# FC2's 64-row chunk as two stacked passes in three of seven products, and b2 added by GpSimd

## The chip, the core and the metric

The kernel runs on one core of a Trainium2 chip. The metric is the time of one execution on the device in microseconds. TensorE (PE, with its weight loads as PEld), VectorE (DVE), ScalarE (ACT), GpSimd (POOL) and SyncE (SP) run side by side, each through its own instructions in order; SP and GpSimd also issue transfers (DMA).

## The reference

Two layers, each of a linear-attention block A and a feed-forward block B, with the same weights in both layers, on 2048 tokens of width D = 640:

```python
x = A_x
for _ in range(2):
    x = x + A(layernorm(x), wqkv, wo)
    x = x + B(layernorm(x), w1, b1, w2, b2)

def B(x, w1, b1, w2, b2):          # D = 640, F = 1728
    h = relu(x @ w1 + b1)
    return (h * h) @ w2 + b2
```

## The kernel before

All matmuls that matter split their float32 operands into a high part (rounded to TensorE's fp32r format) and a low part (the rest), and add three products: high times low, low times high, high times high. `mm3` (line 473) writes this out; FC2 has it at line 1256. ScalarE makes the high part by a copy, VectorE the low part by a subtraction.

**Block B.** Tokens go in NG = 4 groups of 512. For each group FC1 (line 1174) makes 14 chunks of 128 hidden features; chunk 13 has only FL = 64 (1728 = 13 x 128 + 64). `act` puts the squared ReLU into the tile `R`, 128 partitions by 2 halves of the tokens by 2 halves of the chunks by KH = 7 chunks by 256 tokens. So half 1 of the chunks ends in the chunk of 64 rows; its rows 64 to 127 are zero except row 64, which is one (`ones_row`), and the matching row of the second weight matrix holds b2.

FC2 is one level of a Strassen-Winograd scheme on the halves of tokens, chunks and output columns: seven products in the order 1, 5, 6, 2, 7, 3, 4 (`ORDER`). Products 2, 3 and 4 take their weights from, or their activations as, the second half of the chunks, so their last chunk has 64 live rows. Each product goes through PAIRS = 4 units: units 0 to 2 hold two chunks, unit 3 one. `s_op` makes the sums of quadrants of `R` in place on VectorE. `u_hi` and `u_lo` write the high and low parts of a unit into one of five slots of `arena`. `fc2_step` (line 1246) does, for a unit and a tile of 128 tokens, three passes a chunk with 320 output columns; a unit of two chunks has 2 x 2 x 3 = 12 passes, unit 3 has 6, a product 42, a group 294. `fc2_add` adds a finished product to the residual tile `xr[t]` and stores it when it is complete.

**Weights.** In layer 0 the weights are split once and kept in device memory (`kept`), then loaded again for each group: a ring of six tiles `u` (`load_ring`, line 341), and tiles `uw` for unit 0 of each product, which stay (line 351). Class `Prep` does the splitting. For chunk pair p of w2, `load_t` loads chunk p (`a`) and chunk 7 + p (`b`); for the last pair `b` has 64 rows, the rest is zeroed by GpSimd and b2 is loaded into row 64 (line 257). `mix` lets GpSimd form the combinations (line 270), `high`, `low` and `store` split and store them. The last two pairs (`LATE_T`) are prepared during FC1 of layer 0's first group, from steps 0 and 1 on.

**The order of the work** is written out by hand. In block B the events of `at(group, step, f)` run after step `step`; steps 0 to 13 are FC1's chunks, 14 to 41 FC2's units, and events of one step run in the order in which they were entered. `single(g, i)` spreads the preparation of the next group's tile i over group g: loading pq (line 696), its division, the projection in FC1 (steps 4, 7, 10, 13), then `add` (residual and layer-norm statistics, whose last two operations are GpSimd's, lines 371 and 372), `store` (normalise, then a copy to device memory issued by GpSimd, line 405), and loading it back transposed. In layer 0's last group `side_last` loads layer 1's q/k weights (`load_kq`, line 201) and first tiles.

Of the kernel before, what the change touches and what calls it, by code (L numbers as in the profile page):

```python
# [8 lines left out]
F32 = mybir.dt.float32  # L9
R32 = mybir.dt.float32r  # L10
AF = mybir.ActivationFunctionType
ALU = mybir.AluOpType

P = 128
S, D, F = 2048, 640, 1728
# [5 lines left out]
FL = F - 13 * P  # L21
TG = 4
# [14 lines left out]
KH = 7  # L37
PAIRS = 4
ORDER = (1, 5, 6, 2, 7, 3, 4)
# [26 lines left out]
def kernel(  # L66
# [11 lines left out]
    nc = tc.nc  # L78
# [146 lines left out]
    for m in ORDER:  # L225
        for k in range(PAIRS):
            a, b = unit_range(k)
            keep((m, k), [P, 2, b - a, HD])

    class Prep:  # L230
# [20 lines left out]
        def load_t(self, p, at=None):  # L251
            a, b, q = at or (gtile("wa"), gtile("wb"), gtile("wq"))
            nc.sync.dma_start(a, w2[p * P : (p + 1) * P])
            n = P if p < KH - 1 else FL
            if n < P:
                nc.gpsimd.memset(b[n:], 0.0)
                nc.sync.dma_start(b[n : n + 1], b2.rearrange("(o n) -> o n", o=1))
            nc.sync.dma_start(b[:n], w2[(KH + p) * P : (KH + p) * P + n])
            return p, a, b, q

        def mix(self):
            self.raws += self.staged
            self.staged = []
            if not self.mixes:
                return
            p, a, b, q = self.mixes.pop(0)
            lo, hi = slice(0, HD), slice(HD, D)

            def sub(out, x, y, op=ALU.subtract):
                nc.gpsimd.tensor_tensor(out=out, in0=x, in1=y, op=op)  # L270

            sub(q[:, lo], a[:, hi], a[:, lo])
            sub(q[:, hi], b[:, hi], a[:, hi])
            sub(a[:, hi], q[:, hi], a[:, lo], ALU.add)
            self.raws.append(((p, (2, 3)), b, 2 * D))
            self.raws.append(((p, (5, 7)), q, 2 * D))
            self.raws.append(((p, (1, 6)), a, 2 * D))


            def last():  # L280
                sub(b[:, lo], b[:, lo], a[:, hi])

            self.then[p] = last
            self.raws.append(((p, (4,)), b, D))
# [13 lines left out]
        def low(self, n=1):  # L298
            for _ in range(min(n, len(self.halves))):
                key, u, hi, lo, raw = self.halves.pop(0)  # L300
                nc.vector.tensor_tensor(out=lo, in0=raw, in1=hi.bitcast(F32), op=ALU.subtract)  # L301
                self.done.append((key, u))
                if key[1] == (2, 3):
                    self.then.pop(key[0])()
# [231 lines left out]
    for layer in range(N_LAYERS):  # L536
# [6 lines left out]
        ap = sg.enter_context(  # L543
            tc.tile_pool(name=f"a_{layer}", bufs=1, side="left", reuse_waits="tile")
        )
# [73 lines left out]
        if layer == 0:  # L619
# [27 lines left out]
            for ps, a, b in runs:  # L647
                d = T4[0][:, 0, :, a * P : b * P]
                nc.vector.tensor_tensor(
                    out=d[:, 1], in0=ps[:, : (b - a) * P], in1=d[:, 0].bitcast(F32), op=ALU.subtract  # L650
# [16 lines left out]
            out=mask, in_=mask, compare_op=ALU.is_ge, fill=0.0, base=0,  # L667
# [495 lines left out]

        R = bp.tile([P, 2, 2, KH, HT], F32, name="R", tag="R", bufs=1)

        def ones_row(h):
            nc.gpsimd.memset(R[FL:, h, 1, KH - 1], 0.0)
            nc.gpsimd.memset(R[FL : FL + 1, h, 1, KH - 1], 1.0)

        x1_odd["tile"] = bp.tile([P, TG, D], F32, name="x1", tag="x1", bufs=1)  # L1170
        arena = tmp.tile([P, SLOTS, 2, 2, HT], R32, tag="T", name="arena", bufs=2)
        pTs = wtile("pTs").rearrange("p (b j n) -> p b j n", b=2, j=2)

# [56 lines left out]
        def unit(g, n):  # L1230
            q, k = divmod(n, PAIRS)
            a, b = unit_range(k)
            return quad(*QUAD[ORDER[q]], k), arena[:, (g * N_STEPS + n) % SLOTS, :, : b - a]

        def u_hi(g, n):
            v, u = unit(g, n)
            nc.scalar.activation(u[:, 0], v, AF.Copy)  # L1237

        def u_lo(g, n):
            v, u = unit(g, n)  # L1240
            nc.vector.tensor_tensor(out=u[:, 1], in0=v, in1=u[:, 0].bitcast(F32), op=ALU.subtract)  # L1241

        CHAIN = {1: (2, True, False), 6: (2, False, False), 7: (2, False, False), 4: (2, False, True),
# [2 lines left out]
        def fc2_step(g, n, i, first, last):  # L1246
            q, k = divmod(n, PAIRS)
            m = ORDER[q]
            base, opens, _ = CHAIN[m]
            _, u = unit(g, n)  # L1250
            w = wu.get(g, m, k).rearrange("p (j m n) -> p j m n", j=2, n=HD)
            ps = bank(base + i)[:, :HD]
            a, b = unit_range(k)
            for p in range(b - a):
                h, l = (u[:, j, p, i * P : (i + 1) * P] for j in range(2))
                for e, (x, y) in enumerate(((h, w[:, 1, p]), (l, w[:, 0, p]), (h, w[:, 0, p]))):
                    nc.tensor.matmul(  # L1257
                        ps, x, y, start=opens and k == 0 and p == 0 and e == 0,
                        stop=k == PAIRS - 1 and p == b - a - 1 and e == 2, skip_group_check=True,
                    )  # L1260

        ADD = {1: (0, 0), 5: (2, 1), 6: (0, 1), 2: (0, 0), 7: (2, 1), 3: (0, 1), 4: (2, 0)}
# [37 lines left out]
        def at(g, n, f):  # L1300
            events.setdefault((g, n), []).append(f)
# [19 lines left out]
        def single(g, i):  # L1321

            t, b = TG * (g + 1) + i, OUTS[i]

            def on(n, f):
                if n < 0 and g > 0:
                    at(g - 1, NF + N_STEPS + 2 * n, f)
                elif n >= NF:
                    at(g, NF + int(2 * (n - NF)), f)
                else:  # L1330
                    at(g, max(n, 0), f)

            if t > TG:
                on(b - 8, lambda: b_load_pq(t))
            on(b - 6, lambda: b_den(t))
            on(b - 5, lambda: b_blocks(t))
            on(b - 5, lambda: blocks_move(yzp[t], (0, 1)))
            on(b - 4, lambda: blocks_move(yzp[t], (2, 3)))
            sp = p_split(t)
            on(b - 3, lambda: next(sp, None))  # L1340
            on(b - 2, lambda: next(sp, None))
            on(b - 3, lambda: b_load_x(t))
            ps = []

            def out():
                yzp.pop(t)
                for j in range(2):
                    s = slice(j * HD, (j + 1) * HD)
                    ps.append(bank(6 + j)[:, :HD])
                    for c in range(DC):  # L1350
                        a = pT[t][:, :, c * P : (c + 1) * P]
                        mm3(ps[j], a[:, 0], a[:, 1], M[c][:, 0, s], M[c][:, 1, s], c == 0, c == DC - 1)
                pT.pop(t)

            def add():
                for j in range(2):
                    v = xr[t][:, j * HD : (j + 1) * HD]
                    nc.vector.tensor_tensor(out=v, in0=ps[j], in1=v, op=ALU.add)
                ln_stats(("b", t), xr[t])

            def store():
                xn[t] = ftile("xn")
                ln_apply(("b", t), xn[t], xr[t])
                xd[t] = spread_out(xn.pop(t))

            at(g, ("pe", b), out)
            on(b + 1 + 0.5 * (i == 3), add)
            on(b + 2, store)

            def load():  # L1370
                yzx[t] = spread_in(xd.pop(t))

            n = NF + (1, 5, 9, 13)[i]
            at(g, NF + (0, 3, 7, 11)[i], load)
            steps(lambda: x_split(t), (g, n + 4), (g, n + 5), (g, n + 6))

        def ffn_events(g):
            for k in range(PAIRS):
                at(g, 6 + k, lambda k=k: u_hi(g, k))
                at(g, 7 + k, lambda k=k: u_lo(g, k))  # L1380
            for k in range(3):
                at(g, 9 + 2 * k, lambda k=k: s_op(1, k))
            at(g, 11, lambda: u_hi(g, PAIRS))
            at(g, 12, lambda: u_lo(g, PAIRS))
            s = NF
            for h in range(2 if g == 0 else 1):
                at(g, 12 + h if g == 0 else 1, lambda h=h: ones_row(h))
            at(g, s, lambda: s_op(1, 3))
            for n in range(PAIRS + 1, N_STEPS):
                at(g, s + n - 4, lambda n=n: u_hi(g, n))  # L1390
                at(g, s + n - 3, lambda n=n: u_lo(g, n))
            for k in range(PAIRS):
                at(g, s + 3 + k, lambda k=k: s_op(2, k))
                at(g, s + 8 + k, lambda k=k: s_op(3, k))
                at(g, s + 13 + k, lambda k=k: s_op(4, k))
            for q in range(len(ORDER) - 1):
                for i in range(2):
                    at(g, s + PAIRS * (q + 1) + i, lambda q=q, i=i: fc2_add(g, q, i))
# [19 lines left out]
        def side_last():  # L1418
# [21 lines left out]
            for t in range(2):  # L1440
                at(g, s + 8 + 4 * t, lambda t=t: xT_split(t, turn(yz0[t], True)))

        for g in range(NG):
            ffn_events(g)
        for g in range(NG - 1):
# [63 lines left out]
```

## Time and profile before

| | us |
|---|---|
| median of 3 runs | 1326.48 (1326.28 to 1326.78) |
| the profiled execution | 1327.06 |
| its span, first to last instruction | 1325.3 |
| TensorE busy in the span | 1317.7 |
| VectorE, ScalarE, GpSimd busy | 848.4, 735.1, 167.2 |

All times below are from the profiled execution, counted from its first instruction. The granted TensorE clock was 1.00. In rows of groups the numbers are: operation, output and input tiles with shapes, count, then busy us in all and mean ns of one, then idle time in front of it and what ended it. In rows of the timeline: start us, us, engine, line. A row of waits gives us in all, times, longest. In rows of stretches: busy us of PE, PEld, DVE, ACT, POOL with counts, then granted clock, the DMA share (busy share of the 16 transfer engines) and GB/s.

### The profile page before, as it was taken

What the parts mean: (1) busy time and instruction counts of PE and PEld (TensorE: products, weight loads), DVE (VectorE), ACT (ScalarE), POOL (GpSimd) and SP (SyncE); (2) the same over time, 40 slices, a digit from 0 to 9 for tenths busy, and PEclk for the clock granted to TensorE, in tenths of its full rate; (3) what the DMA queues carried; (4) which work ended last, traced back from release to release, by engine and by line L of the source; (5) the groups of instructions that cost most, each with busy time, mean ns of one, the idle gap of its engine ahead of it and who ended that gap; (6) DMA issues with size and microseconds to landing.
All of it is one profiled execution on the core that took longest, in us unless ns stands there. A gap on an engine that the chain in (4) does not pass through costs nothing.

```text
span 1325.3 us, 20933 instructions
## 1 busy us (share of the span) xinstructions
PE 1317.7 (99%) x7525; PEld 1200.1 (91%) x7525; DVE 848.4 (64%) x1575; ACT 735.1 (55%) x1594; POOL 167.2 (13%) x263
## 2 busy tenths in 40 slices
PE   9999999999999999999999999999999999999999
PEld 8888889989988988998988899999899899889888
DVE  8888958757845854833856677686476558458045
ACT  5888967785475467334323233487844744754242
POOL 2333310122001001001012222000110010010000
PEclk9999999999999999999999999999999999999999
DMA  6898994499974985898954456554869569749756
GB/s 198 249 277 272 335 343 142 164 330 380 320 281 148 303 296 169 253 373 287 361 155 127 129 139 169 130 203 158 313 208 350 206 191 323 280 143 297 286 185 216
DMA packets 134751, 320.93 MB, mean 242 GB/s; under 512 B 16679, under 2 KB 61863, under 8 KB 134008
## 3 DMA queue, kind: packets, MB, share of 16 engines
q1 hardware_dynamic: 127416, 297.31, 66.9%
q0 software_dynamic: 7232, 22.29, 6.4%
q8 instruction: 60, 0.98, 0.3%
q14 instruction: 43, 0.35, 0.1%
HBM read 242.16 MB, written 65.54 MB: 232 GB/s over the span
## 4 chain that ended last, share of the span: by engine, by line
PE 85%; DVE 5%; ACT 4%; DMA 3%; issue 1%; SPq 1%; POOL 0%; ACTq 0%; DVEq 0%; POOLq 0%
PE PS L477 30%; PE PS L1257 25%; PE PS L1189 25%; PE PS L504 2%; ACT z L443 1%; PE PS L1030 1%; PE PS L1043 1%; ACT z L463 1%; DMA kq<-kept_kq 1%; DMA pqt<-pq 1%; DVE bn L367 1%; DMA kept<-uprep 1%; DVE uprep L301 0%; PE PS L837 0%; DVE xT L493 0%
## 5 line engine op out<-in xcount | busy, mean ns | idle before, releaser
L1189 PE MATMUL PS<-xTb,u 128*128 128x512 f32 x1640 | 377.1, 389 | 0.4 <-ACT arena L1237 0.3
L1189 PEld LDWEIGHTS PS<-xTb,u 128*128 128x128 f32 x1640 | 306.6, 188 | 63.6 <-ACT arena L1237 0.7
L477 PE MATMUL PS<-kq,xT 128*128 128x320 f32 (+2 forms) x1575 | 285.0, 334 | 1.5 <-DVE xT L493 1.4
L477 PEld LDWEIGHTS PS<-kq,xT 128*128 128x128 f32 x1575 | 250.3, 188 | 29.6 <-DVE xT L493 2.0
L1257 PE MATMUL PS<-u,arena 128*128 128x320 f32 x1692 | 257.2, 309 | 0.0
L1257 PEld LDWEIGHTS PS<-u,arena 128*128 128x128 f32 x1692 | 250.5, 188 | 0.0
L1241 DVE TENSOR_TENSOR arena<-R,arena 128x512 fp32r<-128x512 f32 x224 | 137.4, 617 | 145.6 <-ACT arena L1237 144.6
L1237 ACT ACTIVATE arena<-R 128x512 fp32r<-128x512 f32 x224 | 128.3, 575 | 177.0 <-PE PS L1257 168.0
L443 ACT ACTIVATE z<-y 32x160 f32<-32x160 f32 x512 | 171.1, 334 | 49.8 <-DVE y L434 43.9
L1200 ACT ACTIVATE R<-PS,b1sb 128x512 f32<-128x512 f32 x104 | 71.5, 687 | 131.2 <-PE PS L1189 130.3
L477 PE MATMUL PS<-kh,xh 128*128 128x512 f32 x480 | 124.8, 393 | 0.9 <-DVE kh L781 0.9
L477 PE MATMUL PS<-uM,pTs 128*128 128x320 f32 x720 | 109.4, 309 | 0.0
L477 PEld LDWEIGHTS PS<-uM,pTs 128*128 128x128 f32 x720 | 107.5, 188 | 1.9
L1257 PE MATMUL PS<-uw,arena 128*128 128x320 f32 x660 | 105.9, 309 | 0.0
L371 POOL TENSOR_SCALAR rs<-mv 128x1 f32<-128x1 f32 x64 | 34.8, 544 | 546.3 <-DVE mv L369 546.3
L477 PEld LDWEIGHTS PS<-kh,xh 128*128 128x128 f32 x480 | 87.1, 188 | 16.9 <-DVE kh L781 1.8
L1257 PEld LDWEIGHTS PS<-uw,arena 128*128 128x128 f32 x660 | 99.2, 188 | 0.2
L1218 DVE TENSOR_TENSOR R<-R 128x512 f32<-128x512 f32 (+1 forms) x128 | 78.2, 616 | 27.7 <-ACT R L1201 27.7
L463 ACT ACTIVATE z<-y 32x160 f32<-32x160 f32 x272 | 90.9, 334 | 3.3
L579 ACT ACTIVATE r<-PS 128x512 f32<-128x512 f32 (+1 forms) x64 | 27.6, 434 | 99.8 <-PE PS L477 98.6
L1270 DVE TENSOR_TENSOR x<-PS,x 128x320 f32<-128x320 f32 x112 | 53.6, 484 | 22.6 <-PE PS L1257 22.6
L1201 ACT ACTIVATE R<-R 128x512 f32<-128x512 f32 x104 | 65.8, 633 | 3.3
(129 smaller groups left out, 1209.9 us busy)
## 6 DMA issues: line engine op xcount, KB each, us to landing
u<-kept SPq DMA_DIRECT2D x113, 640.0 KB, 5.9
u<-kept_w SPq DMA_DIRECT2D x104, 640.0 KB, 5.6
u<-kept SPq DMA_DIRECT2D x56, 320.0 KB, 6.0
kept<-uprep SPq DMA_DIRECT2D x49, 320.0 KB, 5.9
z<-xb SPq DMA_DIRECT2D x160, 80.0 KB, 5.5
pqt<-pq SPq DMA_DIRECT2D x32, 320.0 KB, 6.0
acc<-r POOLq DMA_DIRECT2D x28, 320.0 KB, 5.2
uw<-kept SPq DMA_DIRECT2D x14, 640.0 KB, 8.7
```

The source lines that it names most:

```text
L371: nc.gpsimd.tensor_scalar(rs, mv[:, 1:2], LN_EPS, None, op0=ALU.add)
L443: nc.scalar.activation(zv[j * B32 : (j + 1) * B32, :, i, :], yv[i * B32 : (i + 1) * B32, :, j, :], AF.Copy)
L463: nc.scalar.activation(zv[j * B32 : (j + 1) * B32, :, i, :], yv[i * B32 : (i + 1) * B32, j], AF.Copy)
L477: nc.tensor.matmul(ps, a, b, start=first and i == 0, stop=last and i == 2)
L1189: nc.tensor.matmul(ps, a[:, d, :], bb[:, d, :], start=(d, i) == order[0], stop=(d, i) == order[-1],)
L1200: nc.scalar.activation(r, v, AF.Relu, bias=b1sb[:, c : c + 1])
L1201: nc.scalar.activation(r, r, AF.Square)
L1218: nc.vector.tensor_tensor(out=quad(*out, k), in0=quad(*x, k), in1=quad(*y, k), op=op)
L1237: nc.scalar.activation(u[:, 0], v, AF.Copy)
L1241: nc.vector.tensor_tensor(out=u[:, 1], in0=v, in1=u[:, 0].bitcast(F32), op=ALU.subtract)
L1257: nc.tensor.matmul(ps, x, y, start=opens and k == 0 and p == 0 and e == 0, stop=k == PAIRS - 1 and p == b - a - 1 and e == 2, skip_group_c ...
L1270: nc.vector.tensor_tensor(out=v, in0=ps, in1=v, op=ALU.add)
```

## The change

In products 2, 3 and 4 the last chunk's unit becomes one tile of 128 rows: rows 0 to 63 hold the high part, rows 64 to 127 the low part of the same 64 features. The weights of the second half of the chunks get the same 64 high rows twice, and their low tile gets zeros in rows 64 to 127. Two passes, stacked activations times low weights and stacked activations times high weights, then give the three products. Row 64 is no longer free for b2: the ones and the b2 row go, and b2 is loaded once per layer as a broadcast to 128 partitions (`b2bc`, SP) and added to the residual tile by GpSimd, one add of 128x640 for each of 16 token tiles a layer. Tiles of groups 1 to 3 get theirs three steps after their projection, those of group 0 at FC1 steps 4, 6, 8 and 10.

```diff
@@ load_t
                 nc.gpsimd.memset(b[n:], 0.0)
-                nc.sync.dma_start(b[n : n + 1], b2.rearrange("(o n) -> o n", o=1))
@@ mix
             sub(a[:, hi], q[:, hi], a[:, lo], ALU.add)
+            short = p == KH - 1
+            if short:
+                nc.gpsimd.tensor_copy(b[FL:], b[:FL])
...
             def last():
-                sub(b[:, lo], b[:, lo], a[:, hi])
+                if short:
+                    sub(b[:FL, lo], b[:FL, lo], a[:FL, hi])
+                    nc.gpsimd.tensor_copy(b[FL:, lo], b[:FL, lo])
+                else:
+                    sub(b[:, lo], b[:, lo], a[:, hi])
@@ low
-                nc.vector.tensor_tensor(out=lo, in0=raw, in1=hi.bitcast(F32), op=ALU.subtract)
+                if key[0] == KH - 1 and key[1] in ((2, 3), (4,)):
+                    nc.vector.tensor_tensor(
+                        out=lo[:FL], in0=raw[:FL], in1=hi[:FL].bitcast(F32), op=ALU.subtract
+                    )
+                    nc.gpsimd.memset(lo[FL:].bitcast(F32), 0.0)
+                else:
+                    nc.vector.tensor_tensor(out=lo, in0=raw, in1=hi.bitcast(F32), op=ALU.subtract)
@@ block B
-        def ones_row(h):
+        def no_rows(h):
             nc.gpsimd.memset(R[FL:, h, 1, KH - 1], 0.0)
-            nc.gpsimd.memset(R[FL : FL + 1, h, 1, KH - 1], 1.0)
+        b2bc = bp.tile([P, D], F32, name="b2bc", tag="b2bc", bufs=1)
+
+        def f_bias(t):
+            nc.gpsimd.tensor_tensor(out=xr[t], in0=xr[t], in1=b2bc, op=ALU.add)
...
+        def stacked(n):
+            q, k = divmod(n, PAIRS)
+            return k == PAIRS - 1 and ORDER[q] in (2, 3, 4)
@@ u_hi, u_lo
+            if stacked(n):
+                nc.scalar.activation(u[:FL, 0], v[:FL], AF.Copy)
+                return
...
+            if stacked(n):
+                nc.vector.tensor_tensor(
+                    out=u[FL:, 0], in0=v[:FL], in1=u[:FL, 0].bitcast(F32), op=ALU.subtract
+                )
+                return
@@ fc2_step
+                seq = ((h, w[:, 1, p]), (l, w[:, 0, p]), (h, w[:, 0, p]))
+                if stacked(n):
+                    seq = (seq[0], seq[2])
@@ single
             on(b + 2, store)
+            on(b + 3, lambda: f_bias(t))
@@ events, ahead of all others
+        at(0, 0, lambda: nc.sync.dma_start(
+            b2bc, bass.AP(tensor=b2.tensor, offset=b2.offset, ap=[[0, P], [1, D]])))
+        for t in range(TG):
+            at(0, 4 + 2 * t, lambda t=t: f_bias(t))
```

More of the change, by code (lines that the diff above doesn't have):

```diff
@@ L1255, in fc2_step @@
                 h, l = (u[:, j, p, i * P : (i + 1) * P] for j in range(2))
-                for e, (x, y) in enumerate(((h, w[:, 1, p]), (l, w[:, 0, p]), (h, w[:, 0, p]))):
+                seq = ((h, w[:, 1, p]), (l, w[:, 0, p]), (h, w[:, 0, p]))
+                if stacked(n):
+                    seq = (seq[0], seq[2])
+                for e, (x, y) in enumerate(seq):
                     nc.tensor.matmul(
                         ps, x, y, start=opens and k == 0 and p == 0 and e == 0,
-                        stop=k == PAIRS - 1 and p == b - a - 1 and e == 2, skip_group_check=True,
+                        stop=k == PAIRS - 1 and p == b - a - 1 and e == len(seq) - 1,
+                        skip_group_check=True,
                     )
@@ L1386, in ffn_events @@
             for h in range(2 if g == 0 else 1):
-                at(g, 12 + h if g == 0 else 1, lambda h=h: ones_row(h))
+                at(g, 12 + h if g == 0 else 1, lambda h=h: no_rows(h))
             at(g, s, lambda: s_op(1, 3))
```

## The prediction

> **What bounds the kernel now.** I read the page's busy table first, then who TensorE waited for, then the groups of instructions with shapes kept apart, then the chain of work that ended last, and the time-ordered views of the places where a gain could be lost.
>
> ```profile
> span 1325.3 us, 20933 instructions
> PE 1317.7 (99%) x7525; PEld 1200.1 (91%) x7525; DVE 848.4 (64%) x1575; ACT 735.1 (55%) x1594; POOL 167.2 (13%) x263
> ...
> PE PS L625 <- POOL ident masks.py:199: 1.4, 1, 1.4
> PE PS L477 <- DVE xT L493: 1.4, 2, 1.2
> PE PS L477 <- DVE kh L781: 0.9, 2, 0.5
> PE PS L1189 <- ACT arena L1237: 0.3, 1, 0.3
> ...
> L1257 PE MATMUL PS<-u,arena 128*128 128x320 f32 x1692 | 257.2, 309 | 0.0
> L1257 PE MATMUL PS<-uw,arena 128*128 128x320 f32 x660 | 105.9, 309 | 0.0
> ...
> 320.19 43.12 PE PS L1257 x294
> 880.77 13.22 PE PS L504 x90
> ```
>
> TensorE is busy 1317.7 of 1325.3 us and all its listed waits add up to 4.0 us. FC2 (line 1257) has 1692 + 660 = 2352 matmuls, 294 for each of 8 token groups, and no idle time in front of any. In a group the 294 take 43.12 us: 146.7 ns for one pass. So this stage is paced by the number of passes, and a pass that goes is worth 146.7 ns as long as what feeds TensorE keeps up.
>
> **The passes removed.** Unit 3 of products 2, 3 and 4 (the single 64-row chunk) is now two passes instead of three, for two token tiles: 3 x 2 = 6 passes a group, 48 in all. 48 x 146.7 ns = 7.04 us, 0.88 us a group, 0.29 us for each such unit. The two passes left have the same stationary tile one after the other; line 504 does that already (each high or low half meets two column halves) at 13.22 / 90 = 146.9 ns, so a pair costs what two others do. As the last group ends the program, its 0.88 us counts in full too.
>
> **Engines around the stacked unit.** The ScalarE copy and the VectorE subtraction handle 64 rows by 256 instead of 128 by 256. Duration follows the columns (64x512 and 128x512 both take 0.68 us below), so I cost both at zero change. New is that the first pass needs the VectorE half as well, where it needed ScalarE's alone. What hides this is the lead over TensorE:
>
> ```profile
> L1207 DVE SCALAR_TENSOR_TENSOR R<-R 64x512 f32<-64x512 f32 x8 | 5.5, 683 | 0.3
> L1218 DVE TENSOR_TENSOR R<-R 128x512 f32<-128x512 f32 x96 | 65.5, 683 | 27.7 <-ACT R L1201 27.7
> ...
> 324.28 0.63 POOL L405 DMA_DIRECT2D xb<-xn  x1 [1.48 <-DVE xn L377]
> ...
> 342.47 0.65 DVE L1241 TENSOR_TENSOR arena<-R,arena 128x512 fp32r<-128x512 f32 x1
> ...
> 320.00:363.00 43.00, 43.00 (x295) 43.00 (x294) 36.23 (x67) 16.51 (x30) 2.03 (x5) 1.00 1.00 316
> ```
>
> Unit 17 of the first group (fifth product, second unit) is finished by VectorE at 343.12; TensorE starts it at 320.19 + 4 x 6.16 + 1.76 = 346.59 (12 passes are 1.76 us, a product of 42 is 6.16). That is 3.47 us of lead in the fullest FC2 stage (VectorE 36.23 of 43 us). A stacked unit takes 0.29 off it. Cover gone, VectorE's delay would go to TensorE one for one.
>
> **The adds on GpSimd.** 32 adds of b2, 128x640 each. The nearest rows:
>
> ```profile
> L778 POOL TENSOR_TENSOR acc<-acc,r 128x640 f32<-128x640 f32 x2 | 3.6, 1818 | 16.3 <-DMA acc<-r 9.0 <-DVE r L587 7.3
> L773 POOL COPY acc<-r 128x640 f32<-128x640 f32 x2 | 1.8, 906 | 69.7 <-DVE r L587 69.7
> L1168 POOL MEMSET R<- 1x256 f32 x10 | 3.3, 328 | 0.6
> L256 POOL MEMSET R<- 64x640 f32 x1 | 0.6, 628 | 0.1
> ...
> 273.41 2.68 POOL L270 TENSOR_TENSOR R<-R 128x320 f32<-128x320 f32 x3
> 275.32 1.45 DVE L301 TENSOR_TENSOR uprep<-R,uprep 128x640 fp32r<-128x640 f32 x1 [2.90 <-ACT uprep L295]
> L301 DVE TENSOR_TENSOR uprep<-st,uprep 128x640 fp32r<-128x640 f32 x13 | 10.6, 818 | 0.8 <-ACT uprep L295 0.6 <-DMA wa<-in_B_w_dram 0.2
> ```
>
> Same shape and kind: 1.82 us, so 58 us for 32. Ten memsets (3.3 us) go; two copies of the weight preparation (0.9 and, at half the columns, about 0.45 us) and two memsets (0.6 and 0.3) come. GpSimd goes from 167 to about 224 us, idle for most of the span, so its own time is free; queued behind an add are only the layer-norm pair, the copy of the normalised tile to memory and the last mixes, one FC1 step later. The price can be on VectorE. At 275.32 a VectorE subtraction met GpSimd's mixes, which ran to 276.09, and took 1.45 us instead of 0.82: 0.63 lost in 0.77 us of overlap. So an add can hold VectorE for nearly its 1.82 us. In the six FC2 stages with an add (after the copy at 324.28 in the first) that is less than 3.47 - 0.29 us of lead: zero. In FC1 VectorE idles about half of the time and does not feed TensorE directly: zero, except in layer 0's first group.
>
> That rule is also in the Trainium skill (SBUF — State Buffer, § SBUF: two separate sides): the port pair shared by the two engines is an exclusive lock, held for a whole instruction, and whoever comes second blocks fully. The trace agrees, with 0.63 of 0.77 us. For the add's length the GPSIMD Engine Reference (§ Performance versus the Vector engine) has about 2.6 cycles an element at 1.2 GHz, an estimate of 1.39 us for 640; the measured 1.82 us decides, and with 1.39 the loss of the next part would be 2 x 0.43 = 0.9 us smaller at its upper end.
>
> **Layer 0's first group.** Here the weights are still being prepared and everything is tight:
>
> ```profile
> SPq L257 <- POOL R L256: 6.3, 1, 6.3
> ...
> 258.05 0.41 SPq L696 DMA_DIRECT2D pqt<-pq  x1
> ...
> 284.64 0.51 SPq L696 DMA_DIRECT2D pqt<-pq  x1
> ...
> 288.47 0.74 ACT L295 ACTIVATE uprep<-R 128x640 fp32r<-128x640 f32 x1
> ...
> 290.17 0.87 POOL L270 TENSOR_TENSOR R<-R 128x320 f32<-128x320 f32 x1 [2.58 <-DVE uprep L301]
> ...
> 294.02 0.82 DVE L713 TENSOR_TENSOR pr<-pqt,zbc 128x640 f32<-128x640 f32 x1 [2.32 <-DMA pqt<-pq]
> ...
> 313.28 2.52 PE L1189 MATMUL PS<-xTb,u 128*128 128x512 f32 x10 [0.34 <-ACT arena L1237]
> ...
> 265.00:270.00 5.00, 5.00 (x23) 4.13 (x22) 1.27 (x3) 4.86 (x11) 2.35 (x4) 1.00 0.62 212
> 285.00:320.00 35.00, 34.63 (x184) 30.30 (x183) 21.17 (x39) 26.20 (x58) 7.11 (x12) 1.00 1.03 411
> 900.00:974.00 74.00, 74.00 (x396) 65.81 (x395) 42.31 (x81) 52.04 (x120) 8.11 (x17) 1.00 0.65 233
> ```
>
> Removed with the b2 row is a transfer that held SP for 6.3 us until a GpSimd memset was done; the two loads behind it start earlier, into a stretch that is not yet saturated (share 0.62 from 265 to 270). But the next loads wait for VectorE and ScalarE anyway, so I give it nothing. Added is the broadcast of b2, 320 KB, at 411 GB/s 0.8 us of a path that is full (share 1.03) from 285 on; it is issued just ahead of the load at 258.05, some 27 us before that, so probably free. The mix of the last chunk pair comes 2.7 us later (an add and a copy ahead of it): ready near 278.8, needed by ScalarE at 288.5. Then the mix at 290.17, a copy and two adds keep GpSimd until about 290.17 + 0.87 + 0.5 + 2 x 1.82 = 295.2. VectorE's work from 294.02 on, which the chain follows into TensorE's 0.34 us wait at 313.28, may start 1.2 us late. Bounds: the wait vanishes (gain 0.34), or 1.2 + 0.8 = 2.0 us lost. I take 0.5 lost, nearer the gain's end since loads that start earlier work against it. In layer 1's first group the same adds stand beside a data path with a third to spare (share 0.65): zero.
>
> **The layer boundary.**
>
> ```profile
> 624.34 34.33 PE PS L1257 x234
> 658.68 0.32 SPq L341
> ...
> 659.53 10.00 DMA kq<-kept_kq
> 669.58 1.67 PE PS L477 x6
> ...
> 640.00:670.00 30.00, 29.94 (x199) 29.18 (x198) 19.56 (x37) 8.50 (x15) 0.00 (x0) 1.00 0.96 353
> ```
>
> The last q/k weight tile of layer 1 is issued at 659.53, right after TensorE freed a slot at 658.66, and lands at 669.53; TensorE takes it at 669.58. It lands just in time. In the changed kernel one stacked unit lies before the issue (0.29 us earlier), three before the use (0.88 earlier). So TensorE waits 0.88 - 0.29 = 0.59 us that it did not. Bounds: 0 (it lands faster) and 0.88 (the path, 0.96 busy, sets the landing). I take 0.59.
>
> **The sum.** 7.04 - 0.59 - 0.5 = 5.95 us gained. The profiled execution lasted 1327.06 us (1.76 around its span), so 1321.1; the median of the runs shown is 0.58 lower, so 1326.48 - 5.95 = 1320.5. With the terms' ends: 7.04 + 0.34 = 7.4 gained, or 7.04 - 0.88 - 2.0 = 4.2, so 1319.1 to 1322.3.
>
> **Rivals.** (a) Memory sets the pace where its share is near 1.00: in layer 0's first and last FC2 the passes only turn into waits for weights. Those 2 x 0.88 us go, and with 2.0 us lost in the first FC1 the gain is 7.04 - 1.76 - 2.0 = 3.3: 1323.2. For it: shares of 1.00 and 0.96. Against: the four waits above name no weight load in FC2.
>
> (b) Slower: in the six FC2 stages with an add, GpSimd keeps VectorE out longer than the lead. One add, at 1.82 us, does not; it decides from 3.2 us on, and from 3.2 + 7.04 / 6 = 4.4 us the kernel is slower. If an add between back-to-back two-operand subtractions takes three times its length, 5.5 us, TensorE loses 2.3 us six times: 13.8 - 7.04, 1333.2. For it: VectorE runs without a gap there. Against: mixes kept their 0.88 us beside VectorE at 273 to 276.
>
> (c) It does not do what it says: FC2 is paced by units, not passes, so fewer passes only leave TensorE waiting for ScalarE and VectorE: 1326.5. For it: these work only about four units ahead. Against: 0.0 idle in both rows of line 1257, and a product of short and long units advances at 146.7 ns a pass.
>
> **How the numbers follow.** Forecast 0.74, with its own range 1319.1 to 1322.3; (a) 0.14; (b) 0.06; (c) 0.06. The range for 8 in 10 takes in (a): 1318.9 to 1323.3. A measurement here tells about 0.2%, 2.65 us, from no change: faster is below 1323.8, which is the forecast and (a), 0.88; same is (c), 0.06; slower is (b), 0.06.
>
> **What will show it.** Right: each FC2 stage has 288 matmuls and takes 42.24 +- 0.1 us, with no idle time in front of its matmuls; GpSimd's adds show near 1.8 us; the wait before the layer-1 q/k matmuls grows to about 0.6 us, and the one in layer 0's first FC1 to about 0.8. Wrong: FC2 stages that stay at 43 us (then (c)), TensorE waits on weight loads inside FC2 (a), or TensorE waiting for VectorE's arena halves a few us after an add (b).

## The result, and the profile after

The changed kernel takes 1320.20 us (median of 6 runs, 1319.74 to 1320.73), the kernel before beside it 1326.46 us (6 runs, 1326.22 to 1327.84): ratio 0.9951, 95% interval 0.9939 to 0.9964. The profiled execution lasted 1320.5 us, 6.56 us less than that of before.

From the page of the changed kernel the span, the busy table and the two groups of FC2's matmuls (now line 1287):

```profile
span 1318.5 us, 20882 instructions
PE 1310.7 (99%) x7477; PEld 1193.5 (91%) x7477; DVE 865.5 (66%) x1575; ACT 735.5 (56%) x1594; POOL 219.1 (17%) x289
...
L1287 PE MATMUL PS<-u,arena 128*128 128x320 f32 x1644 | 250.2, 309 | 0.0
...
L1287 PE MATMUL PS<-uw,arena 128*128 128x320 f32 x660 | 106.1, 309 | 0.0
```

The view of TensorE's waits (us in all, times, longest) has four rows; the three of 1.4, 1.4 and 0.9 us outside FC1 and FC2 are as before, and one is new in it:

```profile
PE PS L489 <- DMA kq<-kept_kq: 0.2, 1, 0.2
```

TensorE has 48 matmuls less and still no idle time that the groups show in front of FC2's. The 0.3 us in FC1 for which ScalarE was named is gone, 0.2 us for the last q/k tile of layer 1 has come. The wait for that tile is not new, though: the list of the matmuls leaves out most of what their weight loads (PEld) wait. The waits of the weight loads for it, from 600 to 670 us, first before and then after:

```profile
PEld PS L477 <- DMA kq<-kept_kq: 0.5, 1, 0.5
```

```profile
PEld PS L489 <- DMA kq<-kept_kq: 0.6, 1, 0.6
```

VectorE is busy 17.1 us longer although it has the same 1575 instructions.

The chain of waits of the changed kernel (start, length, what ran) shows the stages around layer 0's first FC1 and around the layer boundary:

```profile
255.52 17.02 PE PS L1204 x75
...
306.18 9.09 PE PS L1204 x40
...
319.67 42.24 PE PS L1287 x288
...
621.17 34.24 PE PS L1287 x232
...
656.27 9.57 DMA kq<-kept_kq
665.88 1.67 PE PS L489 x6
```

FC2 of a group is 288 passes in 42.24 us, 0.88 us less than before. The last 10 of the 40 matmuls that close layer 0's first FC1 are not set off from the others any more. Set against the same places of before, stage by stage on TensorE:

| where | before, us | after, us | gained |
|---|---|---|---|
| FC2, 8 stages, passes alone | 8 x 43.12 | 8 x 42.24 | 7.04 |
| FC1 of layer 0's first group | 65.02 | 64.15 | 0.87 |
| start of the program to that FC1 | 253.58 | 253.93 | -0.35 |
| last FC2 of layer 0 and first part of layer 1 | 286.28 | 285.77 | 0.51 (0.88 of it counted above: -0.37) |
| end of the last FC2 to the end of the span | 3.27 | 3.65 | -0.38 |
| around the span | 1.76 | 2.0 | -0.25 |

The 0.37 us at the layer boundary have two parts. In time order, matmuls of that FC2 (start, length, line, count) and VectorE beside them:

```profile
639.49 1.92 PE L1287 MATMUL PS<-uw,arena 128*128 128x320 f32 x12
...
645.35 2.12 PE L1287 MATMUL PS<-uw,arena 128*128 128x320 f32 x12
```

```profile
643.84 0.83 DVE L505 TENSOR_TENSOR xT<-y,xT 128x640 fp32r<-128x640 f32 x1 [0.80 <-ACT xT L502]
...
645.79 0.48 DVE L1301 TENSOR_TENSOR x<-PS,x 128x320 f32<-128x320 f32 x1
```

The same twelve passes take 0.20 us more at 645.35, and between 600 and 670 us the one wait of a weight load in FC2 is for VectorE's addition of line 1301, 0.2 us. So this FC2 takes 42.44 us. The place lies right behind the first stacked unit, that of product 2. TensorE comes to it 0.29 us earlier, and the addition starts 645.79 - 621.17 = 24.62 us into the stage, where before it was 648.70 - 624.34 = 24.36, so 0.26 later. A stacked subtraction costs VectorE more than its duration shows. The same window of VectorE, a subtraction of 128x256 and one of 64x256 with what follows each:

```profile
648.60 0.42 DVE L1268 TENSOR_TENSOR arena<-R,arena 128x256 fp32r<-128x256 f32 x1
648.93 0.42 DVE L1233 TENSOR_TENSOR R<-R 128x256 f32<-128x256 f32 x1
...
651.98 0.42 DVE L1264 TENSOR_TENSOR arena<-R,arena 64x256 fp32r<-64x256 f32 x1
652.43 0.49 DVE L1301 TENSOR_TENSOR x<-PS,x 128x320 f32<-128x320 f32 x1
```

Both last 0.42 us, but the next instruction starts 0.33 us after the first and 0.45 us after the second. In this trace all 24 stacked subtractions start 0.03 us or more after the end of the instruction before and are over 0.03 us before the next begins. Where nothing has to be waited for, most of the 128x256 ones overlap their neighbours by about 0.08 us instead. That is 0.1 us more on each side. The six traces of kernels that stack product 2 all have this wait of 0.20 us, with and without the adds (experiment 2), and the six others have not.

The other part is the wait for the q/k tile: its first use comes 665.88 - 663.61 = 2.27 us after the end of FC2, before it was 669.58 - 667.46 = 2.12, so 0.15 more. This part scatters from kernel to kernel: the weight load waits 0.48 us for the tile before and 0.64 after (the 0.5 and 0.6 above), 0.43 in experiment 2, 0.17 in 3 and 8, and not at all in 1, 4, 5, 6 and both kernels of 7, of which 4, 5 and 6 have the changed FC2.

Together 7.04 + 0.87 - 0.35 - 0.37 - 0.38 - 0.25 = 6.56 us. The spans are given to 0.1 us, so the last two rows hold to about 0.05.

### The profile page after: what moved, and what is told of

The parts are those of the page before. It is cut to its first block, busy times and chain, and to the rows that moved or that the text cites. A ratio compares the mean times of both kernels' runs of the same rounds, so it can differ in the third digit from the quotient of the medians.

```text
span 1318.5 us, 20882 instructions
## 1 busy us (share of the span) xinstructions
PE 1310.7 (99%) x7477; PEld 1193.5 (91%) x7477; DVE 865.5 (66%) x1575; ACT 735.5 (56%) x1594; POOL 219.1 (17%) x289
## 4 chain that ended last, share of the span: by engine, by line
PE 91%; ACT 2%; DVE 2%; DMA 2%; SPq 1%; issue 1%; POOL 0%; ACTq 0%; DVEq 0%; POOLq 0%
PE PS L489 32%; PE PS L1204 28%; PE PS L1287 25%; PE PS L516 3%; ACT z L475 1%; PE PS L1042 1%; PE PS L1055 1%; DMA kq<-kept_kq 1%; SPq L246 1%; PE PS L849 0%; PE PS L637 0%; DMA xt<-in_A_x_dram 0%; DMA kept<-uprep 0%; DVE xT L505 0%; DVE r L599 0%
## 5 line engine op out<-in xcount | busy, mean ns | idle before, releaser
L1287 PE MATMUL PS<-u,arena 128*128 128x320 f32 x1644 | 250.2, 309 | 0.0
L1287 PEld LDWEIGHTS PS<-u,arena 128*128 128x128 f32 x1644 | 243.4, 188 | 0.0
L1268 DVE TENSOR_TENSOR arena<-R,arena 128x512 fp32r<-128x512 f32 (+1 forms) x200 | 140.8, 707 | 135.3 <-ACT arena L1259 134.8
L1259 ACT ACTIVATE arena<-R 128x512 fp32r<-128x512 f32 (+1 forms) x200 | 117.9, 593 | 157.9 <-PE PS L1287 131.9
L598 DVE TENSOR_SCALAR r<-r 128x512 f32<-128x512 f32 (+1 forms) x64 | 21.3, 332 | 70.4 <-ACT r L591 70.2
```

The source lines that it names most:

```text
L1287: nc.tensor.matmul(ps, x, y, start=opens and k == 0 and p == 0 and e == 0, stop=k == PAIRS - 1 and p == b - a - 1 and e == len(seq) - 1, s ...
```

## The experiments

Ten kernels were run, each beside the kernel before on the same chip, in this order of questions: which half of the change gains, whether the gain follows the passes, what an add costs, and what lies behind the small terms of the table.

**1. The bias alone.** Three passes for every unit, b2 by the broadcast and GpSimd's adds:

```diff
-            short = p == KH - 1
+            short = False
...
-                if key[0] == KH - 1 and key[1] in ((2, 3), (4,)):
+                if False:
...
-            return k == PAIRS - 1 and ORDER[q] in (2, 3, 4)
+            return False
```

> Three passes everywhere again, b2 still by broadcast and GpSimd adds. Theory (the gain is the 48 passes and nothing else of size): FC2 stages are back at 294 matmuls in 43.12 us, and the time is that of the kernel before less the 0.34 us wait in layer 0's first FC1: 1326.1 us (1325.8 to 1326.5). Rival 1 (moving b2 out of the matmul brings part of the gain itself, through SP and the removed memsets): below 1324.5. Rival 2 (the adds cost time by locking VectorE out): above 1327.

Measured: 1326.95 us against 1326.25, ratio 1.0006 (0.9998 to 1.0015), above the range expected; of the 0.7 us more, the end of the program and the time around the span account for about 0.6 (experiment 8). Seven FC2 stages take 43.12 us again. The first FC1 still takes 64.15 us, so this gain comes without any stacking; FC2 right behind it takes 43.69 us. From the chain of waits of this kernel:

```profile
339.48 8.53 DMA u<-kept
348.15 15.20 PE PS L1287 x102
...
427.49 43.12 PE PS L1287 x294
```

The weights that are needed at 348 hold TensorE's weight loads for 0.57 us, and the stage is longer by as much: in this execution a late transfer took back one stage later most of what FC1 had saved. Moving b2 gains nothing by itself.

**2. The stacking alone.** Neither broadcast nor adds; b2 is left out of the result:

```diff
         def f_bias(t):
-            nc.gpsimd.tensor_tensor(out=xr[t], in0=xr[t], in1=b2bc, op=ALU.add)
+            return
...
-        at(0, 0, lambda: nc.sync.dma_start(
-            b2bc, bass.AP(tensor=b2.tensor, offset=b2.offset, ap=[[0, P], [1, D]])))
```

> The changed kernel without the broadcast load and without the 32 adds: b2 is left out of the result. Theory (adds are off the path): within 0.3 us of the changed kernel, 1320.2 us, though VectorE's busy time falls back by about 17 us to that of the kernel before (848). Rival (the adds hold VectorE and through it TensorE, or the broadcast delays loads): 1 us or more faster than the changed kernel, below 1319.2.

Measured: 1319.63 us against 1326.25, ratio 0.9950 (0.9938 to 0.9963). FC2 takes 42.24 us as in the changed kernel, and 42.44 at the layer boundary, also as there. The b2 row's load is gone here too, but leaving out that load alone gains nothing (experiment 7), so the whole gain is the stacking's. The gain is 6.62 us here and 6.26 with the adds and the broadcast: they cost some 0.4 us on top (0.6 between the two medians, taken on different chips), a little more than the 0.3 us expected, and it does not lie in FC2. VectorE's busy time falls back to 851.1 us, where about 848 was expected.

**3. One product stacked in place of three.**

```diff
-            return k == PAIRS - 1 and ORDER[q] in (2, 3, 4)
+            return k == PAIRS - 1 and ORDER[q] == 3
```

> Only product 3 stacked: 16 passes fewer instead of 48. Theory (146.7 ns for each pass that goes): 2.35 us from the passes, 0.34 from the first FC1, a loss of up to 0.2 at the layer boundary: 1326.46 - 2.5 = 1324.0 us; FC2 stages of 292 matmuls in 42.83 us. Rival (FC2 is paced by units, or the gain comes from elsewhere): not in proportion, either 1326 or already near 1321.

Measured: 1324.65 us, ratio 0.9988 (0.9979 to 0.9997), 0.65 us above the forecast: 16 passes give 2.35 us, of which 0.41 at the end and 0.32 around the span (experiment 8) are lost again, and 1.60 us were measured. The chain of waits of this kernel up to its first FC2:

```profile
304.56 8.02 DMA u<-kept_w
312.72 2.51 PE PS L1204 x10
...
319.62 42.83 PE PS L1287 x292
```

Two passes less are 43.12 - 42.83 = 0.29 us, so the stage follows the passes: 294, 292 and 288 give 43.12, 42.83 and 42.24 us. The stage is not paced by units. And the FC2 at the layer boundary takes 42.82 us, without the 0.20 us that is lost there behind product 2's stacked unit: product 3 comes after that place. The first two rows bear on the open point of experiment 7: they name the transfer of a weight tile that lands at 312.58 and holds the last ten matmuls of FC1.

**4. Three adds in place of one.** Add, subtract, add again, for one token tile of each of six groups, so that GpSimd keeps at it for three times as long in six FC2 stages:

```diff
-            nc.gpsimd.tensor_tensor(out=xr[t], in0=xr[t], in1=b2bc, op=ALU.add)
+            n = 3 if t >= TG and t % TG == 3 else 1
+            for i in range(n):
+                op = ALU.subtract if i % 2 else ALU.add
+                nc.gpsimd.tensor_tensor(out=xr[t], in0=xr[t], in1=b2bc, op=op)
```

> Changed kernel with the add that falls into FC2 (fourth tile of the next group, six stages) done three times: add, subtract, add. Each stage then has 4.8 us of GpSimd adds instead of 1.6. Theory L1 (an add bars VectorE for its whole length and the next add follows at once): VectorE's subtraction for unit 6 is 5.2 us late, 0.4 us over its lead of 4.8, and the following work goes on being late: 0.4 to 1.5 us lost in each of six stages, 1322.5 to 1329. Theory L2 (VectorE gets one instruction in between two adds): the lead shrinks by about 2 us at the first and by less than the lead in all; TensorE does not wait, 1320.2 us.

Measured: 1324.65 us against 1326.68, ratio 0.9983 (0.9974 to 0.9993). Six FC2 stages take 42.93 to 42.96 us, 0.70 more than with one add, the other two stay as they were. First what one add does in the changed kernel, in order of time (start, length, engine and line, what):

```profile
322.13 0.69 DVE L1268 TENSOR_TENSOR arena<-R,arena 128x512 fp32r<-128x512 f32 x1 [0.54 <-ACT arena L1259]
...
323.89 2.67 DVE L1268 TENSOR_TENSOR arena<-R,arena 128x512 fp32r<-128x512 f32 x1 [0.54 <-ACT arena L1259]
...
324.41 1.59 POOL L1185 TENSOR_TENSOR x<-x,b2bc 128x640 f32<-128x640 f32 x1
...
326.48 0.68 DVE L1233 TENSOR_TENSOR R<-R 128x512 f32<-128x512 f32 x1
327.08 0.41 DVE L1268 TENSOR_TENSOR arena<-R,arena 128x256 fp32r<-128x256 f32 x1
```

Then the same stretch with three adds (lines are three higher there):

```profile
323.85 2.66 DVE L1271 TENSOR_TENSOR arena<-R,arena 128x512 fp32r<-128x512 f32 x1 [0.54 <-ACT arena L1262]
...
324.36 5.58 POOL L1188 TENSOR_TENSOR x<-x,b2bc 128x640 f32<-128x640 f32 x3
...
326.43 2.06 DVE L1236 TENSOR_TENSOR R<-R 128x512 f32<-128x512 f32 x1
328.42 1.80 DVE L1271 TENSOR_TENSOR arena<-R,arena 128x256 fp32r<-128x256 f32 x1
```

One add of 1.59 us stretches a subtraction of 0.69 us to 2.67: VectorE loses 1.98 us. With three adds each stretches one VectorE instruction, by 1.97, 1.38 and 1.39 us, 4.74 in all; between two adds VectorE gets one instruction through. TensorE loses 0.70 of the 4.74, so about 4.0 us of VectorE's delay are covered here. The time lies in theory L1's range, but VectorE's behaviour is theory L2's; what L2 had wrong is the cover. VectorE's stretched subtraction begins 0.52 us before the add's record does (323.89 and 324.41) and is held all the same; as the profiler's spans on GpSimd are rough, which of the two came first is not shown.

**5. Five adds.** The same with `n = 5`:

> The same with five adds, 8 us of GpSimd work in each of six FC2 stages. Theory L1: 3.5 us or more lost in each stage, above 1341 us. Theory L2: VectorE gets four instructions in between in 8 us where it needs about ten; it falls behind by some 5 us, more than the lead of 3.2 to 4.8: 0.5 to 2 us lost in each stage, 1323 to 1332 us. If neither holds (adds give way to VectorE): 1320.2 us.

Measured: 1340.57 us, ratio 1.0101 (1.0086 to 1.0116). That is above theory L2's range and just below L1's. Four of the six stages take 45.27 to 45.29 us; the other two take 46.12 and 46.43 and are the only ones with a granted clock below 1.00, 0.96. Time-ordered view of the first of them, and TensorE's waits in this kernel:

```profile
324.06 2.66 DVE L1271 TENSOR_TENSOR arena<-R,arena 128x512 fp32r<-128x512 f32 x1 [0.54 <-ACT arena L1262]
...
324.57 9.24 POOL L1188 TENSOR_TENSOR x<-x,b2bc 128x640 f32<-128x640 f32 x5
...
326.64 2.06 DVE L1236 TENSOR_TENSOR R<-R 128x512 f32<-128x512 f32 x1
328.63 1.80 DVE L1271 TENSOR_TENSOR arena<-R,arena 128x256 fp32r<-128x256 f32 x1
330.36 2.06 DVE L1236 TENSOR_TENSOR R<-R 128x512 f32<-128x512 f32 x1
...
332.74 1.62 DVE L1271 TENSOR_TENSOR arena<-R,arena 128x512 fp32r<-128x512 f32 x1
```

```profile
PE PS L1290 <- DVE arena L1271: 6.5, 6, 1.1
PE PS L1290 <- DVE x L1304: 4.1, 5, 0.8
```

VectorE loses 1.97 + 1.38 + 1.39 + 1.38 + 0.93 = 7.05 us and the stage 45.27 - 42.24 = 3.03: again 4.0 us covered, and what goes beyond comes through in full. TensorE now waits for VectorE's halves by name. This is the slower rival's mechanism; one add a stage stays 2 us below the point where it begins.

**6. The adds on VectorE.** Same broadcast, same places, other engine:

```diff
-            nc.gpsimd.tensor_tensor(out=xr[t], in0=xr[t], in1=b2bc, op=ALU.add)
+            nc.vector.tensor_tensor(out=xr[t], in0=xr[t], in1=b2bc, op=ALU.add)
```

> Changed kernel with the 32 adds on VectorE instead of GpSimd, at the same places in the order. Theory (VectorE has the time): each add is 0.82 us, 26 us in all against the 17 us that VectorE now loses to the lock; no change on the path, 1320.2 us +- 0.3. Rival (they delay VectorE's in-order work of layer 0's first FC1, where it waits for the broadcast or comes in front of the subtractions): 0.5 to 2 us slower, 1321 to 1322.5.

Measured: 1320.21 us, ratio 0.9947 (0.9931 to 0.9964): no difference from the changed kernel, as expected. The profiled execution, 1321.61 us, is the longest of the four; in it TensorE's weight loads wait 0.78 us for weights at 349.12, in layer 0's first FC2. The row of VectorE's subtractions by shape, in the kernel without b2 (experiment 2) and in the changed one:

```profile
L1267 DVE TENSOR_TENSOR arena<-R,arena 128x512 fp32r<-128x512 f32 x168 | 114.0, 682 | 119.5 <-ACT arena L1258 119.0
```

```profile
L1268 DVE TENSOR_TENSOR arena<-R,arena 128x512 fp32r<-128x512 f32 x168 | 125.7, 751 | 116.7 <-ACT arena L1259 116.2
...
L1185 POOL TENSOR_TENSOR x<-x,b2bc 128x640 f32<-128x640 f32 x32 | 51.9, 1628 | 13.2 <-DMA b2bc<-in_B_b_dram 12.3
```

With the adds on VectorE:

```profile
L1185 DVE TENSOR_TENSOR x<-x,b2bc 128x640 f32<-128x640 f32 x32 | 26.8, 837 | 0.0
```

VectorE is busy 851.1 us without b2, 865.5 with GpSimd's adds and 872.0 with its own. So GpSimd's 51.9 us of adds take 14.4 us of VectorE's time, and sparing VectorE the adds spares it 6.5 of the 20.9 us by which its own adds raise it (872.0 - 851.1).

**7. The stop in layer 0's first FC1: the b2 row's queue, and the row itself.** The prediction had given nothing for the 6.3 us that SP waits in front of the b2 row. In one kernel before, GpSimd issues that load; in the other it is left out, and with it b2:

```diff
-                nc.sync.dma_start(b[n : n + 1], b2.rearrange("(o n) -> o n", o=1))
+                nc.gpsimd.dma_start(b[n : n + 1], b2.rearrange("(o n) -> o n", o=1))
```

> The kernel before, with the b2 row's load issued by GpSimd instead of SP, so that SP no longer waits 6.3 us for GpSimd's memset; nothing else. Theory A (the 0.34 us wait in layer 0's first FC1 went because SP was free earlier): the next weight and pq loads are issued near 264 instead of 269, and the wait at 313 is 0.1 us or less. Theory B (it went for another reason, such as a later or earlier start of the stage): it stays at 0.3 us or more. Time: 1326.1 with A, 1326.5 with B, not to be told apart by the time alone.

```diff
-                nc.sync.dma_start(b[n : n + 1], b2.rearrange("(o n) -> o n", o=1))
```

> The kernel before without the load of the b2 row (the zeroed rows of the product's weight tile stay zero, so b2 is left out of the result); everything else as before, three passes for the 64-row chunk, no broadcast, no adds. What is still open is the stop in FC1 of layer 0's first group, 0.87 us before chunk 13, which stayed when the row went to GpSimd's queue. Theory R (the stop goes with the single-row transfer, on whichever queue): FC1 of that group takes 64.15 us and the kernel gains 0.9 us, 1325.6. Rival S (the stop goes with the order of the transfers between 300 and 313 us on a full path, and the row has no part in it): 65.0 us as before, and 1326.5. Both: FC2 43.12 us in all eight stages, the end after the last FC2 3.44 us.

Measured: with the row on GpSimd's queue 1326.78 us (one run, against 1326.68), FC1 65.02 us as before. SP was indeed free: the same load of SP in order of time, before and then with the row moved:

```profile
268.46 0.54 SPq L341 DMA_DIRECT2D u<-kept_w  x1
```

```profile
263.05 0.33 SPq L341 DMA_DIRECT2D u<-kept_w  x1
```

It goes 5.4 us earlier and nothing is gained, so SP's wait is not the cause. Without the row 1326.32 us, ratio 1.0000 (0.9990 to 1.0009), and FC1 takes 64.41 us: between what the two theories expected, though the time does not fall. Experiment 8, which keeps the row, has 64.53. The chain of waits of the kernel without the row:

```profile
306.20 6.82 PE PS L1188 x30
313.04 2.52 PE PS L1188 x10
```

And of the kernel before (FC1's first 75 matmuls do not lie on its chain; they begin at 255.17):

```profile
312.65 0.53 ACT arena L1237
313.28 2.52 PE PS L1189 x10
```

So the row has at most a small part in the stop. ScalarE's copy, named as the releaser, is not its cause either. The same copy in the changed kernel, in order of time:

```profile
312.86 0.61 ACT L1259 ACTIVATE arena<-R 128x512 fp32r<-128x512 f32 x1
```

It ends at 313.47, and the same ten matmuls start there at 306.18 + 6.82 = 313.00. The trace of experiment 3 names the transfer of a weight tile; for the kernel before that is inferred. The weight load of the ten matmuls stands idle 0.74 us in the kernel before, 0.12 to 0.55 in eight of the ten experiments, and not at all after and in experiments 1 and 4. Where it stands idle it goes on between 312.5 and 313.7 us, and where FC1 began later (255.52 after, 255.17 before, 255.07 to 256.56 in the twelve traces) it has less to wait. So a part of the 0.87 us belongs to the 0.35 us that the first FC1 began later in that execution, in code that the change does not touch; what is kept by the start of FC2 is 320.19 - 319.67 = 0.52 us. Which transfer sets that landing stays open.

**8. The broadcast alone.** The kernel before, with the broadcast load at its place and nothing that reads it:

```diff
+        b2bc = bp.tile([P, D], F32, name="b2bc", tag="b2bc", bufs=1)
...
+        at(0, 0, lambda: nc.sync.dma_start(
+            b2bc, bass.AP(tensor=b2.tensor, offset=b2.offset, ap=[[0, P], [1, D]])))
```

> The kernel before with the broadcast load of b2 added at the place where the changed kernel has it, and nothing that reads it; the b2 row is loaded as before, no adds. Theory Q (the broadcast load makes the end longer, not the adds, since the end was 0.37 us longer with adds on GpSimd and with adds on VectorE): 3.8 us from the last FC2 to the end of the span in place of 3.44. Rival T (the adds do it): 3.44 us. Of the about 0.25 us more around the span, which showed with adds on GpSimd and not with adds on VectorE, theory G (GpSimd's work does it) expects 1.76 us here as before. FC2 43.12 us in all; FC1 of the first group 65.0 us if the single row or the order of the transfers sets the stop.

Measured: 1327.72 us (10 runs), ratio 1.0010 (1.0001 to 1.0020). FC2 takes 43.12 us again and FC1 of the first group 64.53. The end is longer, as theory Q has it (its figures count from a point 0.17 us before that of the table). But not because of the broadcast's data: what sets the end can be read in the last instructions of all twelve traces. In every one the last store is issued 0.03 us after VectorE's last addition, and SP sees it landed 1.81 to 1.83 us after that addition. SP then has to go through the rest of a row of semaphore waits, one each 0.06 us, before the engines meet and the program ends. At which wait of the row the last store stands depends on how many transfers SP has issued in all:

| kernel | SP's transfers | waits behind the last store's | end after the last addition, us |
|---|---|---|---|
| before | 832 | 0 | 2.72 |
| experiment 2, both kernels of 7 | 831 | 1 | 2.78 to 2.79 |
| experiment 8 | 834 | 6 | 3.08 |
| changed, experiments 1, 3, 4, 5, 6, 9 | 833 | 7 | 3.13 to 3.14 |

The change takes one transfer of SP away (the b2 row) and adds two (the broadcast in each layer), and the wait for the last store moves from the last place of the row to the eighth from the end: 3.13 - 2.72 = 0.41 us. By this any other transfer of SP would do the same, but that was not run. The median is 1.4 us longer than before (1327.72 against 1326.32); the profiled execution, 1327.01 us, is the second shortest of the ten, and what makes the others longer still stays open. The 0.25 us around the span go with GpSimd's adds: the median of time less span is 1.72 us before (19 runs), 1.80 here, 1.69 with VectorE's adds and 1.93 to 2.08 in every kernel with GpSimd's. How the adds do it is not shown.

**9. The q/k tile one step earlier.** In the changed kernel, against the wait at the layer boundary:

```diff
-            for c, n in ((1, 5), (2, 13), (3, 21)):
+            for c, n in ((1, 5), (2, 13), (3, 20)):
```

> Changed kernel with layer 1's fourth q/k weight tile loaded after FC2 step 20 instead of 21. Theory (it lands just in time and TensorE gives back 0.35 us there): its issue moves from 656.3 to about 654, it lands about 2 us earlier, the stretch from the start of FC2 of layer 0's last group to the first use of that tile falls from 44.71 to 44.36 us; 1319.8 us. Rival (the transfers are full there, so the landing does not move, or other loads come late instead): 44.7 us or more, no change or slower.

Measured: 1320.93 us, ratio 0.9958 (0.9945 to 0.9970). The chain of waits of this kernel at that place:

```profile
621.30 34.24 PE PS L1287 x232
655.56 7.72 DMA u<-kept
```

The wait for the q/k tile is gone, and FC2's last weights are late instead: that FC2 takes 42.94 us, and with the first part of layer 1 it makes 285.76 us, as in the changed kernel (285.77). So the rival was right: in this execution the order of two transfers only decided which of them TensorE waits for. In experiments 4, 5 and 6, with the order of the changed kernel, it waits for neither.

## Why the prediction was right, point by point

- **Passes, right to the hundredth.** 48 passes at 146.7 ns were to give 7.04 us, and do. The pair with one stationary tile costs what two others do, and the stage follows the passes at 294, 292 and 288. Rival (c), a pace set by units, falls with that.
- **Work on the stacked unit, right in duration, not in cost.** The 64x256 copies of ScalarE take 410 ns, as the 128x256 ones do, and VectorE's subtractions 0.42 us. But these were costed at zero change, and each takes VectorE some 0.2 us more, since it does not overlap the instructions on either side. ScalarE's rows:

```profile
L1259 ACT ACTIVATE arena<-R 128x256 fp32r<-128x256 f32 x32 | 13.1, 410 | 9.1 <-PE PS L1287 7.6 <-DVE R L1233 1.5
...
L1257 ACT ACTIVATE arena<-R 64x256 fp32r<-64x256 f32 x24 | 9.8, 410 | 8.2 <-PE PS L1287 8.2
```

- **The adds, right in effect, a little off in size.** 1.63 us each in place of 1.82, and GpSimd at 219.1 us in place of 224. An add was to hold VectorE for nearly its length and to be covered: it costs VectorE 1.98 us in the fullest stage, more than its own length, and TensorE nothing. The rule of the Trainium skill that was weighed (SBUF — State Buffer, § SBUF: two separate sides) agrees in that one engine is held while the other works, 1.98 us for one add, 4.74 for three, 7.05 for five; who came first is not shown. The estimate of 1.39 us made from the Trainium skill (GPSIMD Engine Reference, § Performance versus the Vector engine) lies below the mean of 1.63 us that they took.
- **The lead, mis-sized on the safe side.** Three adds and five both show 4.0 us of cover in that stage, where the prediction counted 3.47 less 0.29 at another unit. Rival (b) had the mechanism and the sign; its price of 5.5 us for one add did not occur, but 5.58 us of adds in a row cost a stage only 0.70 us, not 2.3: VectorE gets an instruction through between adds, and the cover is larger.
- **Layer 0's first group, the wrong sign.** The step that failed is "VectorE's work from 294.02 on, which the chain follows into TensorE's 0.34 us wait at 313.28, may start 1.2 us late", taken as 0.5 us lost. FC1 there gained 0.87 us, 0.52 net of the later start. The 1.2 us did not come: the subtraction that stood at 296.35 before stands at 296.65 after, 0.30 us later, and the stage began 0.35 later. And the chain had been followed through a releaser that was not the cause: the matmuls start without ScalarE's copy, and in experiment 3's trace the transfer of a weight tile is behind them. The stop in the kernel before is also longer than the 0.34 us of visible idle time, so the bound of 0.34 for a gain was too tight. As the stop scatters over the traces, this gain is in part luck.
- **SP's wait in front of the b2 row, right.** Nothing was given for it, and freeing SP by itself gained nothing (one run).
- **The layer boundary, too large and partly in the wrong place.** The tile did not land just in time: TensorE's weight load already waited 0.48 us for it, which the list of the matmuls' waits does not show. 0.59 us more were to be lost on it, 0.15 were: it is issued 656.27 - 621.17 = 35.10 us into FC2, 0.09 earlier than before (35.19) and not 0.29, as 0.20 us are lost ahead of it, but lands in 9.57 us where it had taken 10.00. Since other kernels with the same FC2 do not wait for it at all, these 0.15 us are no steady cost of the change. The steady part is the 0.20 us inside that FC2, where VectorE's work was costed at zero: its lead had been read in the first FC2 of layer 0, and here it is used up behind the first stacked unit. Rival (a), late weights that turn passes into waits, shows inside FC2 in three traces: at this place in experiment 9 (0.49 us), and in layer 0's first FC2 in experiments 1 (0.57) and 6 (0.78). In the changed kernel's own trace it shows in no FC2, only in the tile's wait.
- **Not foreseen.** 0.38 us at the end, from the number of SP's transfers, and 0.25 around the span, with GpSimd's adds; both come of moving b2. And a start 0.35 us later in code that the change leaves alone, where the twelve traces differ by up to 1.5 us. These three, 0.98 us, stand against what the first FC1 did better than forecast (0.87 + 0.5 = 1.37) and the layer boundary (0.22). So the profiled gain of 6.56 us against 5.95 comes of terms of both signs; 1320.2 against 1320.5 us is closer than the terms were, and that is luck. Without the terms that scatter, 7.04 - 0.20 - 0.41 - 0.25 = 6.2 us are left, and the medians differ by 6.26.

## What to carry to other kernels

Where a stage is paced by matmul passes and nothing idles in front of them, a pass removed is worth its time exactly, and a short contraction chunk is the place to look for one. A second engine's work beside VectorE is free only up to VectorE's lead, so find that lead by adding work until the stage gets longer, not by reading one unit's. Read the waits of the weight loads beside those of the matmuls, which hide a part of them. A short idle time in front of a matmul does not tell its cause: look at a second kernel in which the named releaser is late and see whether the matmul still waits for it.

## What the runs showed of the hardware

- GpSimd's 128x640 additions hold up VectorE's two-operand instructions: one add of 1.59 us made a 0.69 us subtraction last 2.67 us; in a row of adds of 1.85 us each (9.24 / 5), one VectorE instruction gets through between two.
- Handing 32 additions to GpSimd spared VectorE 6.5 us of the 20.9 us by which its own adds raise it (872.0 against 851.1): the rest comes back as longer VectorE instructions.
- A VectorE subtraction that reads rows 0 to 63 and writes rows 64 to 127 (64x256) lasts 0.42 us like one of 128x256, but the next instruction starts 0.45 us after it, not 0.33, and it does not overlap the one before either.
- The end of this program depends on how many transfers SP has issued: with 831 to 834 of them the last store, landed 1.81 to 1.83 us after the last addition in all, is followed by 0 to 7 more waits of 0.06 us, and the end comes 2.72 to 3.14 us after that addition.
